# Layer-norm transposes, row sums and transposed reciprocals as column strips of 32

## The chip, the core and the metric

The kernel runs on one core of a Trainium2 chip. TensorE (PE in the profile) multiplies matrices, ScalarE (ACT) takes the exponentials, VectorE (DVE) does element-wise work, GpSimd (POOL) and SyncE (SP) mostly start transfers. The metric is the device time of one execution in microseconds; lower is better. Three runs of the kernel before gave 2268.7, 2272.3 and 2274.1 us, median 2272.32.

## The reference

Four transformer attention blocks follow each other on an input of 2048 tokens by 640 features, with 32 heads of 20 features. Blocks 0 and 2 use windowed causal attention (256 keys back), blocks 1 and 3 see all keys.

```python
def block(x, wqkv, wo, windowed):
    h = (x - mean(x)) / sqrt(var(x) + 1e-5)        # per token
    q, k, v = split_heads(h @ wqkv)                # 32 heads of 20
    s = q @ k.T * 20 ** -0.5
    if windowed:
        s = where((i - j >= 0) & (i - j < 256), s, -1e9)
    return x + merge_heads(softmax(s) @ v) @ wo
for w in (A, B, A, B):
    x = block(x, w.wqkv, w.wo, windowed=(w is A))
```

## The kernel before, in words

All four blocks are woven into one stream that is written out when the program is built. The outer loop goes over *tiles* of up to three banks of scores (128 keys by 512 queries each). In each turn TensorE writes the scores of one tile (line 1305), ScalarE takes exponentials (line 1336), and TensorE multiplies older exponentials by the values (line 1369). Scores alternate between two sets of banks, so TensorE may be about one tile ahead of ScalarE.

A *unit* is four heads by 512 queries. Four heads lie side by side in one matrix of 128 partitions, each in 32 of them: 20 or 21 are used. So scores use 32 rows of TensorE's array ("32*128" in the profile), the values use 21 columns ("128*21"), and the helper `by_columns` (line 297) splits all projections into four column strips of 32 ("128*32").

Between the scores and the values of a turn, `pump` lets *tasks* advance by a planned credit: the layer norm `t_ln`, projections, the tails of finished units. The heat counter adds filler matmuls (`unread`, which calls `by_columns` on the identity and a mask) wherever the planned work of TensorE is low, to keep its clock up. All of this is fixed when the program is written out; nothing is chosen at run time. Within an engine the order is the program's, and between engines semaphores bind.

Three places matter for the change.

- `t_ln` (transposes at line 432) normalises 128 tokens into `xn`, writes filler into the bank, turns the five 128-column pieces of `xn` around by TensorE, and `evac` copies them into `xnT`. There are 15 such layer norms of four groups of tokens; the first layer norm has its own code and isn't changed.
- `t_tail`, first step (line 1042): for one or two finished units, a matmul with four columns (`sel4`) per head group and 128 queries picks the row sums out of `oT`. VectorE takes reciprocals `rz` and splits them into a high and a low part in `hl`.
- `t_tail`, second step (line 1059): `hl` is transposed into `rp`, copied to `rT`, and later spread over the partitions (line 1080) and multiplied in (line 1084).

Of the kernel before, what the change touches and what calls it, by code (L numbers as in the profile page):

```python
# [15 lines left out]
P = 128  # L16
# [30 lines left out]
def kernel(  # L47
# [10 lines left out]
    nc = tc.nc  # L58
# [33 lines left out]
    ident = big.tile([P, P], BF16, name="ident", tag="ident")  # L92
    nhalf = big.tile([P, 4], F32, name="nhalf", tag="nhalf")
    sel4 = big.tile([P, 4], BF16, name="sel4", tag="sel4")
# [21 lines left out]
    for h in range(2):  # L116
        for n in range(2):
            a = n * D + h * HD
# [10 lines left out]
    def load_wop(w, dense):  # L129
# [9 lines left out]
        out=ident[:], in_=ident[:], compare_op=ALU.not_equal, fill=1.0,  # L139
# [6 lines left out]
    for m, b, ge in (  # L146
# [6 lines left out]
            out=v, in_=v, compare_op=ALU.is_ge if ge else ALU.is_gt, fill=0.0,  # L153
# [109 lines left out]
    def take_m():  # L263
        while True:
            b = min(mfree, key=mfree.get)
            if mfree[b][0] <= state["tick"]:
                mfree[b] = (1 << 30, 0)
                return b
            yield ("wait", 1)

    def drop_m(b):
        mseq[0] += 1
        mfree[b] = (state["tick"] + (not state["early"]), mseq[0])
# [19 lines left out]
    def by_columns(out_, lhsT, rhs, start, stop):  # L293

        for j in range(4):
            r = slice(32 * j, 32 * j + 32)
            nc.tensor.matmul(out_[r], lhsT=lhsT[:, r], rhs=rhs, start=start, stop=stop)  # L297
# [4 lines left out]
    def room(*tags):  # L302
        while any(live[t] + tags.count(t) > cap[t] for t in tags):
            yield ("wait", 1)
        for t in tags:
            live[t] += 1
        state["running"].holds = True
# [8 lines left out]
    def evac(out_, in_):  # L316
        if state["act"]:
            nc.scalar.copy(out=out_, in_=in_)
        else:
            nc.vector.tensor_copy(out=out_, in_=in_)  # L320
# [7 lines left out]
    def get_w(l, n, c, i):  # L328

        t = wqkp.tile([P, KD, P], BF16, name="wqk", tag="wqk")  # L330
        wtick[l, n, c, i] = state["tick"] + 4
        if l or c:
            a = n * D + i * P
            nc.gpsimd.dma_start(out=t[:], in_=wq_view[l % 2][:, :, a : a + P])
            return t
        tv = t[:].rearrange("p c (j m) -> p c j m", j=4)
        nc.gpsimd.memset(tv[:, :, :, DH:32], 0.0)
        src = raw[:, :, n * D + 80 * i : n * D + 80 * (i + 1)]
        nc.vector.tensor_copy(
            out=tv[:, :, :, 0:DH], in_=src.rearrange("p c (j e) -> p c j e", j=4)  # L340
        )
        wtick[l, n, c, i] = 0
        return t
# [46 lines left out]
    def t_ln(l, c):  # L390
        while ("x", l, c) not in ready:
            yield ("wait", 1)
        yield from room("xnT", "ln")
        for n in (1, 0):
            order = worder[l, n]
            if order and not any(e in wtiles for e in order):
                wtiles[order[0]] = get_w(*order[0])
        users[l, c] = 9 if (l, c) == (0, 0) else (11, 12, 11, 11)[l]
        mv = mvs.pop((l, c))
        rstd = lnp.tile([P, 4], F32, name="rstd", tag="rstd")  # L400
        nc.gpsimd.tensor_scalar(  # L401
            out=rstd[:], in0=mv[:, :, 1], scalar1=EPS, scalar2=1.0, op0=ALU.add, op1=ALU.mult
        )
        nc.gpsimd.tensor_tensor(out=rstd[:], in0=rstd[:], in1=nhalf[:], op=ALU.pow)
        yield ("wait", 2)
        nmr = lnp.tile([P, 4], F32, name="nmr", tag="nmr")
        nc.vector.scalar_tensor_tensor(
            out=nmr[:], in0=mv[:, :, 0], scalar=-1.0, in1=rstd[:], op0=ALU.mult, op1=ALU.mult
        )
        xt = xtp.tile([P, KD, C], BF16, name="xnT", tag="xnT")  # L410

        def normed(i):
            xn = xnp.tile([P, D], BF16, name="xn", tag="xn")
            nc.vector.tensor_scalar(
                out=xn[:], in0=x_sb[:, 4 * c + i, :],
                scalar1=rstd[:, i : i + 1], scalar2=nmr[:, i : i + 1],
                op0=ALU.mult, op1=ALU.add,
            )
            return xn

        rows = deque([normed(0)])
        yield ("wait", 1)
        for i in range(4):
            if i < 3:
                rows.append(normed(i + 1))
            xn = rows.popleft()
            mb = yield from take_m()
            for _ in range(1+(l<2)):
                unread(mb)
            trp = ps[:, mb, :].bitcast(BF16)[:, 0 : KD * P].rearrange("p (c m) -> p c m", c=KD)  # L430
            for dc in range(KD):
                nc.tensor.transpose(  # L432
                    out=trp[:, dc, :], in_=xn[:, dc * P : (dc + 1) * P], identity=ident[:]
                )
            evac(xt[:, :, i * P : (i + 1) * P], trp)
            drop_m(mb)
            yield ("pe", 0.4)
        xnT[l, c] = xt
        live["ln"] -= 1
        ready.add(("xnT", l, c))  # L440
# [192 lines left out]
    def unread(b):  # L633

        by_columns(ps[:, b, :], ident, masks[:, 0, :], True, True)
        state["heat"] += 1.0

    def warm_bank(b):

        if cool() and (  # L640
            state["credit"] <= 0.0 or all(task.wake > state["tick"] for task in todo)
        ):
            unread(b)
# [379 lines left out]
    def t_tail(us):  # L1023
        final = us[-1][0:3] == (3, NC - 1, G - 1)

        def fill(count):

            for n in range(count * final):
                nc.tensor.matmul(
                    ps[:, 0, :], lhsT=ident[:], rhs=masks[:, 0, :], start=True, stop=True  # L1030
                )

        n = len(us)
        yield ("wait", 2)
        fill(2)
        mb = yield from take_m()
        warm_bank(mb)
        zp = ps[:, mb, 0 : 16 * n]
        for i, (l, c, g, oT) in enumerate(us):
            for qb in range(4):  # L1040
                a = 16 * i + 4 * qb
                nc.tensor.matmul(  # L1042
                    zp[:, a : a + 4], lhsT=oT[:, qb * P : (qb + 1) * P],
                    rhs=sel4[:], start=True, stop=True,
                )
        rz = rzp.tile([P, 2, 16], F32, name="rz", tag="rz")[:, 0:n, :]
        nc.vector.reciprocal(out=rz.rearrange("p u r -> p (u r)"), in_=zp)
        drop_m(mb)

        hl = rzp.tile([P, 2, 2, 16], BF16, name="hl", tag="hl")[:, 0:n]  # L1050
        nc.vector.tensor_copy(out=hl[:, :, 0, :], in_=rz)
        nc.vector.tensor_tensor(out=hl[:, :, 1, :], in0=rz, in1=hl[:, :, 0, :], op=ALU.subtract)
        yield ("pe", 0.25)
        fill(3)
        yield ("wait", 2)
        mb = yield from take_m()
        warm_bank(mb)
        rp = ps[0 : 32 * n, mb, :].bitcast(BF16)[:, 0:P]
        nc.tensor.transpose(
            out=rp, in_=hl.rearrange("p u n r -> p (u n r)"), identity=ident[:]  # L1060
        )
        rT = rzp.tile([64, P], BF16, name="rT", tag="rT")
        nc.vector.tensor_copy(out=rT[0 : 32 * n], in_=rp)
        drop_m(mb)
        yield ("pe", 0.1)
        fill(1)
        yield ("wait", 2 if state["tick"] < last_tick[0] else 1)
        for i in range(n):
            yield from scaled(*us[i], 32 * i, rT, fill)
        if any(packed(l, c) for l, c, g, oT in us):  # L1070
            yield ("wait", 2)
        for u in us:
            yield from settle(*u)
# [121 lines left out]
    with tc.manual_schedule():  # L1195
# [14 lines left out]
        n = 0  # L1210
        last_layer = sum(len(u.banks) for u in units[: index[3, 1, 0, None]])
        placed = {}
        while n < last_layer:
            size = 2 if len(tiles) % 2 and narrow(banks[n][0]) else 3
            u = banks[n][0]
# [52 lines left out]
        while ended is None or t < ended + 8:  # L1268
# [3 lines left out]
            if t < len(tiles) or banks:  # L1272
# [9 lines left out]
                for b in cur:  # L1282
                    u = b[0]
# [18 lines left out]
                for n in range(2):  # L1302
                    for i, (u, j, m, b0, subs, first, last, end) in enumerate(cur):
                        for kc, q0, qn, col in subs[n : n + 1]:
                            nc.tensor.matmul(  # L1305
                                sp[:, i, col * P : (col + qn) * P],
                                lhsT=u.k(kc, j), rhs=u.q(j, q0, qn), start=True, stop=True,
# [22 lines left out]
                i = 0  # L1330
                while i < n_b:
                    b0 = cur[i][3]
                    k = i
                    while k < n_b and cur[k][3] == b0:
                        k += 1
                    nc.scalar.activation(  # L1336
                        out=pt[:, i:k, b0 * P :], in_=sp[:, i:k, b0 * P :],
                        func=ACT.Exp, scale=SCALE,
                    )
                    i = k  # L1340
# [5 lines left out]
                r = rate(t)  # L1346
# [6 lines left out]
            for n in range(2 if n_b == 0 or t > closed + 1 else 0):  # L1353
                u = pts[0][3][0] if pts else None
# [11 lines left out]
                for m, (kc, q0, qn, col) in enumerate(subs):  # L1366
                    for _, pg, i, b in group:
                        j = b[1]
                        nc.tensor.matmul(  # L1369
                            op[32 * j : 32 * j + VW, q0 * P : (q0 + qn) * P],  # L1370
                            lhsT=u.v(kc, j), rhs=pg[:, i, col * P : (col + qn) * P],
                            start=(first and m == 0), stop=(last and m == len(subs) - 1),
                            skip_group_check=u.windowed,
                        )
                if end and u.aside:
                    pair = side_done(u)
                    for n, j in enumerate(u.aside):
                        nc.tensor.matmul(  # L1378
                            op[32 * j : 32 * j + VW, :], lhsT=u.v(NT - 1, j),
                            rhs=pair[n // 2][:, n % 2, :], start=False, stop=True,  # L1380
# [12 lines left out]
            if t > 0 and masked is not None:  # L1393
                cur_, pt_ = masked
                i = 0
                while i < len(cur_):
# [4 lines left out]
                    if m == 1 and cur_[0][0].l == 0:  # L1401
                        for b in (1, 2):
                            if b < b0:
# [3 lines left out]
                                out=v, in_=v, compare_op=ALU.is_gt if b == 1 else ALU.is_ge, fill=0.0,  # L1407
# [3 lines left out]
                    elif m is not None:  # L1411
# [5 lines left out]
                            out=pt_[:, i:k, cols], in0=pt_[:, i:k, cols], in1=mv_, op=ALU.mult  # L1417
                        )
                    i = k
# [36 lines left out]
```

The softmax here doesn't subtract the row's maximum and nothing guards it: scores larger than these inputs give would overflow.

## Time and profile before

| what | value |
|---|---|
| span of the profiled execution | 2267.0 us |
| TensorE busy | 1973.3 us (87%) |
| ScalarE busy | 2166.5 us (96%) |
| VectorE busy | 1269.8 us (56%) |
| mean granted TensorE clock | 0.993 |
| exponentials, line 1336 | 1,636 instructions, 2089.3 us |
| transposes, line 432 | 300 matmuls, 28.4 us |
| row sums, line 1042 | 512 matmuls, 22.7 us |
| transposed reciprocals, line 1059 | 65 matmuls, 15.8 us |

A line of the profile's timeline gives the start and the time up to the last end of one or more instructions of one kind, the engine, the line, and what is written from what is read. A shape such as `128*32 128x512` means 128 rows and 32 columns of the array in use, with a moving operand of 128 partitions by 512 elements. Busy times of TensorE include the way through the array, which overlaps with what follows; the distance between starts tells what a matmul costs the next one.

### The profile page before, as it was taken

The numbers are of one execution on the slowest core, as the hardware profiler recorded it, in microseconds if no ns is written. First come the engines' busy times: TensorE is split into PE (matmuls) and PEld (weight loads), VectorE is DVE, ScalarE is ACT, GpSimd is POOL, SyncE is SP. The second block draws the span as 40 slices with busy tenths as digits, with TensorE's granted clock in tenths as the row PEclk, the third lists the DMA queues.
The fourth block names the chain that finished last, engine by engine and source line by source line (L and its number), as shares of the span: only waits on it lengthen the run. The fifth ranks groups of instructions, "written<-read, shape, count | busy, mean of one in ns | idle before, by whom it ended". The sixth has DMA issues, their size and how long they took to land.

```text
span 2267.0 us, 65801 instructions
## 1 busy us (share of the span) xinstructions
PE 1973.3 (87%) x28523; PEld 776.0 (34%) x28524; DVE 1269.8 (56%) x2158; ACT 2166.5 (96%) x1740; POOL 326.2 (14%) x571
## 2 busy tenths in 40 slices
PE   8999998988888888888888988898888888888887
PEld 3444343334333333333333443342322222222222
DVE  6766575435554565555564644442566666656665
ACT  7789899999999989999899999999999999999998
POOL 4454334201100122001210022002000000000000
PEclk9999999999999999999999999999999999999999
DMA  6233223422210233002330033103211111111100
GB/s 195 72 91 94 74 87 93 100 76 50 78 34 15 60 88 104 17 28 58 93 90 15 16 106 105 31 17 91 65 51 31 31 40 34 31 31 43 42 21 16
DMA packets 88384, 136.80 MB, mean 60 GB/s; under 512 B 20766, under 2 KB 63486, under 8 KB 88094
## 3 DMA queue, kind: packets, MB, share of 16 engines
q1 hardware_dynamic: 68878, 79.43, 12.6%
q0 software_dynamic: 19216, 53.17, 8.0%
q8 instruction: 223, 3.65, 0.7%
q14 instruction: 67, 0.55, 0.1%
HBM read 99.52 MB, written 27.79 MB: 56 GB/s over the span
## 4 chain that ended last, share of the span: by engine, by line
ACT 49%; PE 23%; issue 17%; DVE 9%; POOL 1%; DMA 1%; SPq 0%; ACTq 0%; DVEq 0%; POOLq 0%
ACT pt L1336 47%; PE ps L297 14%; PE ps L1305 5%; PE ps L1369 2%; DVE pt L1416 1%; ACT ka L1336 1%; DVE x_sb L562 1%; DVE st L320 1%; DVE on L1084 1%; PE ps L432 1%; PE ps L1080 0%; DVE vs L320 0%; DVE va L320 0%; PE ps L1042 0%; DVE raw_o L909 0%
## 5 line engine op out<-in xcount | busy, mean ns | idle before, releaser
L1336 ACT ACTIVATE pt<-ps 128x1536 bf16<-128x1536 f32 (+2 forms) x1636 | 2089.3, 1462 | 64.8 <-PE ps L1305 56.2
L297 PE MATMUL ps<-masks,ident 128*32 128x512 bf16 x6452 | 553.2, 388 | 113.2 <-ACT pt L1336 59.1
L1305 PE MATMUL ps<-qt,kt 32*128 32x512 bf16 x4004 | 545.7, 384 | 85.5 <-ACT pt L1336 77.6
L1369 PE MATMUL ps<-pt,vt 128*21 128x512 bf16 x3844 | 392.2, 382 | 0.1
L1305 PEld LDWEIGHTS <-kt 32*128 32x128 bf16 x4004 | 163.4, 91 | 544.1 <-issue 526.8
L297 PEld LDWEIGHTS <-ident 128*32 128x32 bf16 x6452 | 162.0, 94 | 361.6 <-issue 350.4
L1416 DVE TENSOR_TENSOR pt<-pt,masks 128x1024 bf16<-128x1024 bf16 (+6 forms) x331 | 191.0, 604 | 154.9 <-ACT pt L1336 154.1
L297 PE MATMUL ps<-xnT,wqk 128*32 128x512 bf16 x3320 | 221.7, 385 | 17.1 <-DVE st L320 7.9
L320 DVE CAST st<-ps 128x512 bf16<-128x512 f32 x134 | 92.6, 691 | 188.1 <-PE ps L297 187.7
L909 DVE TENSOR_SCALAR xnT<-ps 128x512 int32<-128x512 f32 x92 | 63.6, 691 | 191.4 <-PE ps L902 191.3
L297 PE MATMUL ps<-wop,on 128*32 128x320 bf16 x3712 | 156.9, 301 | 13.3 <-DVE x_sb L562 8.4
L1305 PE MATMUL ps<-qa,ka 32*128 32x384 bf16 (+2 forms) x1408 | 117.9, 276 | 32.0 <-ACT pt L1336 29.4
L1369 PEld LDWEIGHTS <-vt 128*21 128x21 bf16 x3956 | 102.5, 91 | 110.4 <-issue 64.8
L1084 DVE TENSOR_TENSOR on<-on,ps 128x512 bf16<-128x512 bf16 x128 | 86.3, 683 | 67.0 <-PE ps L1080 65.3
L297 PE MATMUL ps<-wv,xnT 128*32 128x320 bf16 x2560 | 112.4, 301 | 10.8 <-DVE on L1084 3.3
L297 PEld LDWEIGHTS <-wqk 128*32 128x32 bf16 x3320 | 79.1, 96 | 112.8 <-issue 59.4
L562 DVE TENSOR_TENSOR x_sb<-x_sb,ps 128x320 bf16<-128x320 bf16 x120 | 58.0, 483 | 104.9 <-PE ps L297 104.7
L297 PEld LDWEIGHTS <-on 128*32 128x32 bf16 x3712 | 92.8, 96 | 65.9 <-issue 49.2
L856 DVE CAST on<-ps 128x512 bf16<-128x512 f32 x112 | 77.0, 687 | 59.9 <-PE ps L1378 32.9
L401 POOL TENSOR_SCALAR rstd<-mv 128x4 f32<-128x4 f32 x15 | 3.8, 253 | 712.4 <-DVE mv L388 702.8
L1305 PEld LDWEIGHTS <-ka 32*128 32x128 bf16 x1408 | 43.2, 92 | 117.0 <-issue 110.9
L1369 PE MATMUL ps<-pt,va 128*21 128x384 bf16 (+2 forms) x1408 | 76.9, 281 | 4.6 <-POOL pt L1406 3.5
(100 smaller groups left out, 1589.8 us busy)
## 6 DMA issues: line engine op xcount, KB each, us to landing
vt<-v_d SPq DMA_DIRECT2D x48, 336.0 KB
kt<-k_d SPq DMA_DIRECT2D x192, 80.0 KB
wqk<-in_B_wqkv_dram POOLq DMA_DIRECT2D x80, 160.0 KB, 3.6
wqk<-in_A_wqkv_dram POOLq DMA_DIRECT2D x70, 160.0 KB, 3.3
k_d<-st POOLq DMA_DIRECT2D x75, 128.0 KB, 2.2
q_d<-st POOLq DMA_DIRECT2D x75, 128.0 KB, 2.2
qt<-q_d SPq DMA_DIRECT2D x384, 20.0 KB
v_d<-vs POOLq DMA_DIRECT2D x16, 336.0 KB, 3.4
```

The costliest lines, as they stand in the source:

```text
L297: nc.tensor.matmul(out_[r], lhsT=lhsT[:, r], rhs=rhs, start=start, stop=stop)
L320: nc.vector.tensor_copy(out=out_, in_=in_)
L401: nc.gpsimd.tensor_scalar(out=rstd[:], in0=mv[:, :, 1], scalar1=EPS, scalar2=1.0, op0=ALU.add, op1=ALU.mult)
L432: nc.tensor.transpose(out=trp[:, dc, :], in_=xn[:, dc * P : (dc + 1) * P], identity=ident[:])
L562: nc.vector.tensor_tensor(out=xv, in0=had, in1=yp, op=ALU.add)
L856: nc.vector.tensor_copy(out=oT, in_=op)
L909: V.tensor_scalar(out=xi.bitcast(I32)[:, i * C : (i + 1) * C], in0=side["psum"], scalar1=SCALE * LOG2E * E23, scalar2=-128.0 * E23, op0=AL ...
L1084: nc.vector.tensor_tensor(out=oT, in0=oT, in1=zb, op=ALU.mult)
L1305: nc.tensor.matmul(sp[:, i, col * P : (col + qn) * P], lhsT=u.k(kc, j), rhs=u.q(j, q0, qn), start=True, stop=True,)
L1336: nc.scalar.activation(out=pt[:, i:k, b0 * P :], in_=sp[:, i:k, b0 * P :], func=ACT.Exp, scale=SCALE,)
L1369: nc.tensor.matmul(op[32 * j : 32 * j + VW, q0 * P : (q0 + qn) * P], lhsT=u.v(kc, j), rhs=pg[:, i, col * P : (col + qn) * P], start=(first ...
L1416: nc.vector.tensor_tensor(out=pt_[:, i:k, cols], in0=pt_[:, i:k, cols], in1=mv_, op=ALU.mult)
```

## The change

The three kinds of matmuls that used all columns of the array (or 64 of them) are written as strips of 32 columns, as the projections, the filler and the values are already. Its purpose is that TensorE keeps one shape where it goes from filler to transposes or from tails to values. The products are the same; a transpose of 128 columns becomes four of 32, a row-sum matmul becomes four, and the transposed reciprocals of two units become one strip for each unit.

```diff
@@ t_ln
             for dc in range(KD):
-                nc.tensor.transpose(
-                    out=trp[:, dc, :], in_=xn[:, dc * P : (dc + 1) * P], identity=ident[:]
-                )
+                for j in range(4):
+                    a = dc * P + 32 * j
+                    nc.tensor.transpose(
+                        out=trp[32 * j : 32 * j + 32, dc, :], in_=xn[:, a : a + 32],
+                        identity=ident[:],
+                    )
@@ t_tail, row sums
                 a = 16 * i + 4 * qb
-                nc.tensor.matmul(
-                    zp[:, a : a + 4], lhsT=oT[:, qb * P : (qb + 1) * P],
-                    rhs=sel4[:], start=True, stop=True,
-                )
+                by_columns(zp[:, a : a + 4], oT[:, qb * P : (qb + 1) * P], sel4[:], True, True)
@@ t_tail, transposed reciprocals
         rp = ps[0 : 32 * n, mb, :].bitcast(BF16)[:, 0:P]
-        nc.tensor.transpose(
-            out=rp, in_=hl.rearrange("p u n r -> p (u n r)"), identity=ident[:]
-        )
+        for i in range(n):
+            nc.tensor.transpose(
+                out=rp[32 * i : 32 * i + 32], in_=hl[:, i].rearrange("p n r -> p (n r)"),
+                identity=ident[:],
+            )
```

## The prediction

> **What bounds the kernel now.** I read the busy line of each engine first, then the shares of the chain that ended last, then who waits for whom, and last the chain and TensorE's own order around the three places that change.
>
> The page's busy lines and its chain (part 1 and part 4; times in us, share of the span, number of instructions):
>
> ```profile
> PE 1973.3 (87%) x28523; PEld 776.0 (34%) x28524; DVE 1269.8 (56%) x2158; ACT 2166.5 (96%) x1740; POOL 326.2 (14%) x571
> ...
> ACT 49%; PE 23%; issue 17%; DVE 9%; POOL 1%; DMA 1%; SPq 0%; ACTq 0%; DVEq 0%; POOLq 0%
> ```
>
> ScalarE is 96% busy, nearly all with the exponentials of line 1336; TensorE is second. The waits say how the two hand the lead to each other (waiter, line waited for, us in total, times, longest):
>
> ```profile
> PE ps L1305 <- ACT pt L1336: 107.1, 332, 1.0
> PE ps L297 <- ACT pt L1336: 59.1, 126, 0.9
> ACT pt L1336 <- PE ps L1305: 56.2, 114, 2.2
> ```
>
> TensorE stands 166 us for ScalarE, and ScalarE 56 us for TensorE. So ScalarE leads over most of the span, and TensorE's time counts only in stretches where it has fallen behind. By stretch: in 0 to 300 us ScalarE is busy 249 of 300 us, in 300 to 900 us 585 of 600, in 1500 to 2256 us 751 of 756. The 56 us is about the most that any relief of TensorE can return directly.
>
> The changed groups (busy us, mean ns of one, then idle):
>
> ```profile
> L432 PE MATMUL ps<-ident,xn 128*128 128x128 bf16 x300 | 28.4, 228 | 1.2 <-DVE xn L414 1.2
> L1042 PE MATMUL ps<-sel,on 128*128 128x4 bf16 x512 | 22.7, 166 | 0.7 <-DVE st L320 0.5 <-DVE raw_o L593 0.2
> L1059 PE MATMUL ps<-ident,hl 128*64 128x128 bf16 x63 | 15.3, 243 | 1.0 <-DVE st L320 1.0
> ```
>
> These durations hold the way through the array, which overlaps with the next matmul; the cost is read from start to start, in TensorE's timeline (start, us, what):
>
> ```profile
> 323.16 0.62 PE L297 MATMUL ps<-masks,ident 128*32 128x512 bf16 x8
> 323.70 0.45 PE L432 MATMUL ps<-ident,xn 128*128 128x128 bf16 x5
> ...
> 308.26 0.35 PE L1042 MATMUL ps<-sel,on 128*128 128x4 bf16 x8
> 308.54 0.40 PE L1369 MATMUL ps<-pt,vt 128*21 128x512 bf16 x4
> ...
> 310.93 0.24 PE L1059 MATMUL ps<-ident,hl 128*64 128x128 bf16 x1
> 311.11 0.40 PE L1369 MATMUL ps<-pt,vt 128*21 128x512 bf16 x4
> ```
>
> "128*32" means that an instruction uses all 128 rows of the array and 32 columns. Four such strips run at once: the eight of 323.16 start as four at 323.156 to 323.166 and four at 323.382 to 323.393, so four strips with 512 columns of moving data take 0.22 us. The second four would be through at 323.60, but the 128*128 transposes start at 323.70: about 0.1 us is lost where the shape changes. The same loss stands after the eight of L1042: they start 25 ns apart, the last at 308.447, and the strips of L1369 start at 308.540. Over all changes of shape without a semaphore wait the trace's median gap is 93 to 106 ns. I use 95.
>
> **What the Trainium skill says.** "TensorEngine Tiling (Array Packing)", Key Properties: changing the tiling mode, not just the tile, drains TensorE. The trace agrees: 95 ns at a change, 0 to 4 ns between strips. "TensorE: Matmul & The Clock Gate", Part 3, lets tiles of one mode start about 4 ns apart; here they start 2 to 4 ns apart. The same page, Part 1, has a floor of about 25 ns between starts however small the moving side is; the 25 ns of L1042 agree for full matmuls, and no row of before shows small strips. Its weight path section ties the fast load to 128 columns, so strips lose it; the records show no longer load, 95 ns for 32 columns against 98 for 128.
>
> **The change part by part.** ScalarE's, VectorE's, GpSimd's and SyncE's instructions keep kinds and order; the filler matmuls, planned when the program is written out, stay too. Four places on VectorE wait for ScalarE as well, for work that is long done by then: nothing. On TensorE 2,499 loads with as many matmuls come on top (900 + 1,536 + 63), mostly starting in the shadow of the three strips beside them. TensorE has issued at 19 ns per instruction over 400 in a row, and a fuller issue queue is no bound as long as matmuls average 35 ns per instruction: nothing.
>
> I went along TensorE's order and noted the shape before and after each block.
>
> - Transposes, L432: 60 blocks of 5. 45 lie between strips, 15 between strips before and score matmuls (32 rows) after. Changes gone: 45 x 2 + 15 = 105, by 95 ns: -10.0 us. The transposes themselves start 56 ns apart; four strips with 128 moving columns also do (first four of line 1369 at 302.444, second four at 302.500). So 5 x 56 ns stays.
> - Row sums, L1042: 65 blocks, 44 between strips, 18 with strips after only, 2 with strips before only, 1 beside full-array filler: 108 changes, -10.3 us. Against it 8 matmuls become 8 fours. Best case 25 ns a four, as now. Worst by the nearest row: the weights of four strips were loaded and used between 302.446 and 302.508, 62 ns a four, which gives 8 x (62 - 25) = 0.3 us a block, 19 us in all. I take 37 ns, since the loads should overlap with the 25 ns floor: +0.1 us x 64 = +6.4 us.
> - Transposed ends, L1059: 33 blocks between strips, 29 with strips on one side, 3 with neither: 95 changes, -9.0 us. One 64-column matmul took 174 ns up to the next start, so 80 without the change; two strips take 56: -24 ns x 63 = -1.5 us.
>
> TensorE's sum: -29.3 + 6.4 - 1.5 = -24 us (-31 to -12).
>
> What of it lies on the path? The chain of waits shows such blocks (start, us, what):
>
> ```profile
> 335.13 0.29 PE ps L1042 x8
> 335.42 0.33 PE ps L1369 x4
> ...
> 337.40 0.17 PE ps L1059
> ```
>
> Counted over the span, 38 of the 60 transpose blocks, 26 of 65 row-sum blocks and 16 of 65 ends lie on it. With 1.75, 1.66 and 1.46 changes a block that is 38 x 1.75 x 0.095 = 6.3, 26 x 1.66 x 0.095 = 4.1 and 16 x 1.46 x 0.095 = 2.2: 12.6 us at most. The chain won't shorten one for one, because ScalarE runs just beside it. So I went along the trace with a rule: each change gone puts TensorE ahead, a wait for ScalarE at the scores or filler takes the lead away, and only where ScalarE waited for TensorE first is the lead passed on, up to that wait. It passes on 8.9 us if small strips cost nothing more, 7.2 us at 0.1 us a block, 5.4 us at 0.3 us. More than half comes before 500 us, where ScalarE has its gaps. I take 7.2: 2272.3 - 7.2 = 2265.
>
> **The rivals.**
>
> - Hidden (0.22): the relieved TensorE only waits more for ScalarE. For it: 166 us of such waits, and a ScalarE at 99% after 1500 us. Against it: 85 us of the span before 1500 us in which ScalarE is not busy. Also, TensorE's granted clock fell to half seven times between 91 and 2088 us, for 3.4 to 6.8 us each; one such dip more costs up to 1.7 us of TensorE's work. A gain of 1 to 2 us is left: 2271.
> - Slower (0.10): the floor of 25 ns holds for each small strip. Then 32 x 25 = 0.8 us stands for 0.2: 64 x 0.6 = +38 us, less the 10.3 us of changes, +28 us on TensorE. If half passes on, +14, less 0.3 x 20.5 = 6 of the other two parts: 2280. Against it: all strips seen start 2 to 4 ns apart.
> - The whole chain shortens (0.06): 12.6 us and no new wait: 2260.
>
> My forecast, part of the saving passed on, has 0.62.
>
> **How the numbers follow.** The case of 0.62 spans 2262 to 2269 with the cost of small strips, and nearly all of it is under 2267.8, which is 0.2% down: with the whole chain 0.65 for faster. Hidden and the forecast's upper edge give 0.25 for no difference; slower 0.10. The range leaves out the lower half of the last rival and most of the slow one: 2259 to 2275.
>
> **What would show it.** After: no gap of 95 ns between filler and transposes; transposes, sums and ends under the line of the strip helper; row-sum fours 25 to 62 ns apart, which settles the largest unknown; TensorE's wait for ScalarE up by 10 to 20 us, ScalarE's for TensorE down by some 5. Wrong would be fours of 100 ns, a gap that stays though both sides are strips, or more dips of the clock.

## The result and the profile after

The changed kernel took 2262.07 us (median of 4 runs, 2257.4 to 2263.83) against 2273.11 us for the kernel before (4 runs, 2268.7 to 2274.12). The ratio is 0.9952 with a 95% interval of 0.9931 to 0.9973. Two later comparisons of the same pair (e1 and e12 below) gave 0.9963 (0.9951 to 0.9974; 22 runs) and 0.9975 (0.9961 to 0.9989; 7 runs). So the measured gain is 6 to 11 us; the forecast was 7 us less, 2265 us.

The busy line and the chain's shares of the changed kernel's page:

```profile
PE 1949.7 (86%) x31022; PEld 778.5 (34%) x31023; DVE 1269.8 (56%) x2158; ACT 2163.5 (96%) x1740; POOL 324.8 (14%) x571
...
ACT 51%; PE 21%; issue 16%; DVE 10%; POOL 1%; DMA 1%; ACTq 0%; SPq 0%; DVEq 0%; POOLq 0%
```

TensorE has 2,499 matmuls more and is busy 23.6 us less; all other engines have the same count of instructions. Its share of the chain fell from 23 to 21%, ScalarE's rose from 49 to 51%. The groups that took the place of the old ones (line, operation, shapes, count, busy us and mean ns):

```profile
L434 PE MATMUL ps<-ident,xn 128*32 128x128 bf16 x1200 | 28.6, 225 | 1.6 <-DVE xn L414 1.6
L297 PE MATMUL ps<-sel,on 128*32 128x4 bf16 x2048 | 24.8, 166 | 0.9 <-DVE st L320 0.5 <-ACT xnT L318 0.2 <-DVE raw_o L596 0.2
L1060 PE MATMUL ps<-ident,hl 128*32 128x128 bf16 x128 | 14.8, 223 | 1.1 <-DVE st L320 1.1
```

Four times as many matmuls have nearly the same busy time (the row sums 2.1 us more), because the busy time of concurrent strips is counted once. TensorE's timeline at one site of each kind (start, us, what):

```profile
319.80 0.61 PE L297 MATMUL ps<-masks,ident 128*32 128x512 bf16 x8
320.24 0.45 PE L434 MATMUL ps<-ident,xn 128*32 128x128 bf16 x20
...
303.68 0.36 PE L297 MATMUL ps<-sel,on 128*32 128x4 bf16 x32
303.90 0.40 PE L1371 MATMUL ps<-pt,vt 128*21 128x512 bf16 x4
...
306.34 0.23 PE L1060 MATMUL ps<-ident,hl 128*32 128x128 bf16 x2
306.35 0.44 PE L1371 MATMUL ps<-pt,vt 128*21 128x512 bf16 x4
```

At these sites, eight filler strips held TensorE for 0.54 us before, until the transposes started; now they hold it for 0.44 us, which is their streaming time. The row sums hold it for 0.22 us in place of 0.28. Over all 63 blocks of two units, the groups of four strips start 25 ns apart in the median, 48 ns at most.

Where strips follow without a wait, the median distance from a block's first start to the next matmul fell from 383 to 279 ns for the transposes (37 sites), from 283 to 224 ns for the row sums (45 sites) and from 173 to 7 ns for the reciprocals (36 sites). The last figure flatters, because the reciprocals use two of the four strips. At the 35 sites where four strips follow, two of these start 7 and 11 ns after the block's first start, and the other two 56 and 60 ns after it; before, all four started at 173 to 183 ns. Over the whole trace TensorE changes shape 3,362 times in place of 3,670, the 308 of the prediction.

The waits of TensorE for ScalarE and the other way round (waiter, line, us, times, longest):

```profile
PE ps L1307 <- ACT pt L1338: 115.7, 356, 1.0
PE ps L297 <- ACT pt L1338: 64.9, 146, 0.9
ACT pt L1338 <- PE ps L1307: 56.5, 107, 2.7
```

The first two rose from 166 to 181 us. TensorE is busy 23.6 us less, but the profiled execution is only 5.0 us shorter. So 18.6 us went into idle time, 14 of them into these two waits for ScalarE. The third line didn't fall, though the span did. In the profile of e1, the same kernel at a granted clock of 0.994 in place of 0.991, it is 51.0 us, so dips of the clock are the likely reason.

### The profile page after: what moved, and what is told of

The parts are those of the page before. It is cut to its first block, busy times and chain, and to the rows that moved or that the text cites. A ratio compares the mean times of both kernels' runs of the same rounds, so it can differ in the third digit from the quotient of the medians.

```text
span 2262.0 us, 70803 instructions
## 1 busy us (share of the span) xinstructions
PE 1949.7 (86%) x31022; PEld 778.5 (34%) x31023; DVE 1269.8 (56%) x2158; ACT 2163.5 (96%) x1740; POOL 324.8 (14%) x571
## 4 chain that ended last, share of the span: by engine, by line
ACT 51%; PE 21%; issue 16%; DVE 10%; POOL 1%; DMA 1%; ACTq 0%; SPq 0%; DVEq 0%; POOLq 0%
ACT pt L1338 49%; PE ps L297 14%; PE ps L1307 4%; PE ps L1371 2%; DVE pt L1418 1%; ACT ka L1338 1%; DVE st L320 1%; DVE on L1086 1%; DVE x_sb L565 1%; DVE va L320 1%; PE ps L434 0%; PE ps L1082 0%; DVE xnT L320 0%; DVE vs L320 0%; DVE raw_o L912 0%
## 5 line engine op out<-in xcount | busy, mean ns | idle before, releaser
L1338 ACT ACTIVATE pt<-ps 128x1536 bf16<-128x1536 f32 (+2 forms) x1636 | 2087.2, 1472 | 63.4 <-PE ps L1307 56.5
L297 PEld LDWEIGHTS <-on 128*32 128x32 bf16 x5760 | 118.1, 96 | 78.3 <-issue 55.3
L297 PEld LDWEIGHTS <-xnT 128*32 128x32 bf16 x2560 | 63.5, 95 | 48.6 <-issue 37.7
```

The costliest lines, as they stand in the source:

```text
L1338: nc.scalar.activation(out=pt[:, i:k, b0 * P :], in_=sp[:, i:k, b0 * P :], func=ACT.Exp, scale=SCALE,)
```

## The experiments

ScalarE, VectorE and GpSimd keep their instruction counts in all of them. Beside the measured ratio to the kernel before, the table has the gain at equal granted clock. This is worked out from the runs. Over all runs of the twelve kernels and of the kernel before, a clock of 0.001 less goes with 1.56 us more (one slope for all), and the times of each kernel and of the kernel before are set to a clock of 0.992 with it. The standard error of a gain is 0.2 to 0.6 us. The kernel before is at 2270.8 us by this count, on each of the three chips used within 0.1 us. What a kernel does to the clock itself is taken out by it as well, which matters for e9 and e11.

| kernel | ratio (95%) | runs | mean clock | at equal clock, us |
|---|---|---|---|---|
| e1 all three | 0.9963 (0.9951 to 0.9974) | 22 | 0.9922 | -7.6 |
| e12 all three | 0.9975 (0.9961 to 0.9989) | 7 | 0.9911 | -7.3 |
| e2 transposes | 0.9979 (0.9970 to 0.9988) | 22 | 0.9920 | -5.3 |
| e3 row sums | 0.9996 (0.9984 to 1.0008) | 13 | 0.9910 | -1.3 |
| e4 ends | 0.9993 (0.9981 to 1.0005) | 14 | 0.9916 | -2.0 |
| e5 early | 0.9981 (0.9966 to 0.9997) | 17 | 0.9914 | -5.6 |
| e6 late | 1.0002 (0.9990 to 1.0014) | 14 | 0.9920 | -0.2 |
| e7 full filler | 0.9989 (0.9977 to 1.0000) | 14 | 0.9924 | -2.1 |
| e8 rest as well | 0.9972 (0.9961 to 0.9982) | 19 | 0.9925 | -7.0 |
| e9 filler early | 0.9970 (0.9955 to 0.9985) | 6 | 0.9945 | -2.3 |
| e10 filler late | 1.0001 (0.9989 to 1.0012) | 14 | 0.9911 | -0.7 |
| e11 less filler | 0.9984 (0.9972 to 0.9997) | 14 | 0.9895 | -7.0 |

### The parts, one at a time

All three together (e1):

> All three parts, once more, as the yardstick for the parts on the same chip. Theory A (TensorE saves 95 ns for each of 308 changes of the array's shape, and passes on the part that falls where it leads): with row-sum strips now seen at 25 to 28 ns a four, the carry rule of the prediction gives 8.9 us less. Theory B (the gain is the granted clock, not the changes): the gain follows the granted clock of the runs and is near zero at the same clock.

The transposes alone (e2), the first hunk of the diff:

> Only the layer norms' transposes as strips (105 of the 308 changes gone). A: 5 us less, over half of the gain for a third of the changes, because these blocks lie mostly where TensorE leads (0 to 500 us). B: no order among the parts, all near zero at the same clock. C (what counts is only the number of changes): 3 us less, as for each third.

The row sums alone (e3), the second hunk:

> Only the row sums as strips (108 changes gone). A: 2 us less. C: 3 us less. Slow-strip rival of the prediction (0.8 us a block): 8 us more; the trace of the changed kernel already speaks against it.

The transposed reciprocals alone (e4), the third:

> Only the transposed reciprocals as one strip for each unit (95 changes gone). A: 2 us less. C: 3 us less.

The transposes give 5.3 us at equal clock, 4.8 by the plain ratio; the two others give 1.3 and 2.0 at equal clock, while their plain intervals can't tell them from nothing. The order is theory A's (5, 2, 2), not a third each, though each has about a third of the changes. The gains don't follow the clock, which is within 0.001 of the kernel before's 0.9916 in all four: B falls as the cause of the gain. It does explain most of the scatter of single runs: of e1, the runs at a clock of 0.988 took 2268.6 and 2269.3 us, the runs at 0.995 2256.8 to 2257.9.

### Early and late

The three parts written both ways, chosen by the turn of the outer loop. For e5:

```diff
+if state["tick"] < 330:
     strips of 32
+else:
     as before
```

and for e6 with `>= 330`.

> All three parts as strips, but only in the first 330 turns of the outer loop (about the first 450 us; 85 of the 308 changes gone); later blocks as before. A (passed on where TensorE leads): 5.5 us less, over half of the gain. C (only the number of changes counts): 85/308 of the gain, some 3 us.

> The same from turn 330 on (223 of the 308 changes gone). A: 3.4 us less. C: 223/308 of the gain, some 8 us.

85 changes gone early bring 5.6 us of their 8.1 (85 x 95 ns). 223 changes gone late bring nothing that can be seen, of 21 us; C would have them bring most. Where the late saving went stands in e6's waits:

```profile
PE ps L1324 <- ACT pt L1355: 115.5, 358, 1.0
PE ps L297 <- ACT pt L1355: 64.3, 144, 0.9
```

They sum to 180 us, 14 more than before the change and as many as with all three parts everywhere. The late relief only makes TensorE wait longer for ScalarE. Theory A's 3.4 us for it was too much. The traces agree: e6 and the kernel before have the same dips of the clock (stretches in which it is recorded as half) up to 800 us, and in the start of the same exponential e6 is 0.3 us ahead at 456 us and 0.7 at 786.

The same comparison of the kernel before with e1, along the span:

| before, at us | 370 | 456 | 786 | 926 | 1337 | 1756 | 2255 |
|---|---|---|---|---|---|---|---|
| e1 is ahead by us | 4.8 | 5.5 | 5.8 | 7.7 | 8.0 | 9.6 | 10.3 |

At 370 us both executions had spent 20.5 us at half clock, so the 4.8 us can be put to the change. More than half of the whole is there at 456 us. Of what comes later, 1.9 us come between 786 and 926 us, and 0.9 between 1618 and 1756: the kernel before had its clock at half for 3.4 us at 839 and at 1706 us there, and e1 hadn't. The first at least is no work of the change, since e12, the same kernel as e1, has such a dip at 836 us.

### Shape changes put back, without touching the three parts

```diff
 def unread(b):
-    by_columns(ps[:, b, :], ident, masks[:, 0, :], True, True)
+    nc.tensor.matmul(ps[:, b, :], lhsT=ident[:], rhs=masks[:, 0, :], start=True, stop=True)
     state["heat"] += 1.0
```

> The changed kernel, with each filler of four strips by 512 columns written as one full-array matmul by 512 columns (a filler's product is not used). The streaming time is the same; counted in TensorE's order there are 3902 changes of shape in place of 3362, 540 more, 51 us of TensorE's time at 95 ns each. If the change of shape is what costs (A): slower than the changed kernel, by 15 us at the carry rule's share of 0.3 and by 25 us if half is passed on. If strips as such made the gain, or the clock (B): within 3 us of the changed kernel.

It is 5.5 us slower than e1 at equal clock (ratios 0.9989 and 0.9963), where 15 to 25 were expected: the sign was right, the size far off. The shape changes do cost about what was said, as in this piece of e7's timeline:

```profile
900.16 0.38 PE L638 MATMUL ps<-masks,ident 128*128 128x512 bf16 x1
900.47 0.40 PE L1373 MATMUL ps<-pt,va 128*21 128x384 bf16 x8
```

One full-array filler of 512 columns follows another after 0.215 to 0.227 us in this trace, but the values start 0.31 us after it. Over 487 sites where another shape follows without a wait the median is 0.309 us, so a change costs 0.08 to 0.09 us here. But most of the added changes stand where TensorE waits anyway. First e1's waits, then e7's:

```profile
PE ps L1307 <- ACT pt L1338: 114.2, 352, 1.0
PE ps L297 <- ACT pt L1338: 64.9, 146, 0.9
ACT pt L1338 <- PE ps L1307: 51.0, 108, 2.1
...
PE ps L1309 <- ACT pt L1340: 76.1, 211, 1.0
PE ps L297 <- ACT pt L1340: 58.8, 134, 0.9
ACT pt L1340 <- PE ps L1309: 57.2, 118, 2.1
```

TensorE's waits for ScalarE fell to 135 us from e1's 179. 44 of the 51 us went out of waits and 7 remain, near the 5.5 measured. Place explains this too: only 45 of the 540 added changes lie before 450 us, 4.3 us at 95 ns each, and at 456 us, with 23.9 us of half clock in both executions, e7 is 3.4 us behind e1. The 495 later ones, 47 us of TensorE's time, put it at most 6.1 us further behind. The expectation of 15 to 25 us took the share passed on from blocks that lie elsewhere.

### What is left to convert

```diff
 def t_before_last(): ...
-    nc.tensor.matmul(yp, lhsT=on[0:n, b, ...], rhs=wop[0:n, b, ...], ...)
+    by_columns(yp, on[0:n, b, ...], wop[0:n, b, ...], b == 0, b == 3)
 def fill(count): ...
-    nc.tensor.matmul(ps[:, 0, :], lhsT=ident[:], rhs=masks[:, 0, :], start=True, stop=True)
+    by_columns(ps[:, 0, :], ident, masks[:, 0, :], True, True)
```

> The changed kernel, with the partial output projection before the last unit and the closing filler as strips too (13 more changes gone, 1.2 us of TensorE, nearly all at the end where ScalarE leads). A: within 1 us of the changed kernel.

It is 0.6 us from e1 at equal clock, and no better. None of the other versions beats the changed kernel by more than the measurement can tell.

### More and less of TensorE's time, without a change of shape

In these three, fillers are added or left out ahead of the transposes.

```diff
 for _ in range(1+(l<2)):
     unread(mb)
+if l < 2:       # e9; in e10: if l >= 2
+    by_columns(ps[:, mb, :], ident, masks[:, 0, :], True, True)
```

> The changed kernel with one more filler of four strips (0.216 us, no change of shape) ahead of the transposes of each of the 28 groups of tokens of layers 0 and 1 (51 to 415 us of the trace). TensorE's time up by 6.0 us where it is held to lead. A, as the late half of the change has corrected it (all of it counts before some 450 us, nothing after): slower than the changed kernel by 4 to 6 us, so about 4 us less than before the change. If place doesn't matter (a share of a third everywhere): slower by 2 us.

> The same with the 32 groups of layers 2 and 3 (535 to 1511 us): TensorE's time up by 6.9 us where ScalarE is held to lead. A as corrected: within 1 us of the changed kernel. Place doesn't matter: slower by 2 us.

```diff
-for _ in range(1+(l<2)):
-    unread(mb)
+unread(mb)
+if l < 2:
+    state["heat"] += 1.0
```

> The changed kernel with one filler of four strips in place of two ahead of the transposes of layers 0 and 1 (28 fillers, 6.0 us of TensorE's time gone; the plan still counts them, so that no other filler takes their place). A as corrected: 4 to 6 us faster than the changed kernel, if TensorE's clock holds; if the fillers are what holds it, the granted clock falls, by 0.001 for each 4.5 us at half speed, and some 1.6 us of the gain go for each 0.001.

e9 did as expected at equal clock, and e11 didn't. The plain ratios hide this, because the clock moved. With more filler early, e9 had a mean clock of 0.9945 and took the time of e12 (0.9970 and 0.9975). With less, e11 had 0.9895 and a ratio of 0.9984. The kernel before had 0.9917 on this chip. So the filler ahead of the early transposes seems to hold the clock, by 2.7 standard errors in each direction. At equal clock e9 is 5.0 us slower than e12, of the 6.0 added. e11, for which 4 to 6 us less were expected, is 0.3 us from e12, within the error.

The traces show the same without an adjustment. At 456 us the profiled executions of e1, e9 and e11 have each spent 23.9 us at half clock. In the start of the same exponential, e9 is then 6.0 us behind e1, all that was added; e11 is 0.3 us ahead, of 6.0 taken off. TensorE's idle time before 456 us is 43.8 us in e1 and 48.3 in e11; the increase is spread over waits for the layer norm's `xn` and for ScalarE. So the corrected theory A, that all of TensorE's time before some 450 us counts, failed for time taken off the changed kernel. Perhaps the change has used up what TensorE could pass on at these blocks; that is argued, not shown.

e10 is a plain miss: 6 us slower than e12 where at most 1 was expected. Set beside e8, which had the same dips of the clock before 400 us in its profiled execution (at 50, 90, 220, 244, 258 and 381 us), it is 7.0 us behind in the start of the same exponential by 1756 us. Steps of about 2 us each lie at dips which e8 didn't have (579 and 1343 us) and one of about 1 us in its favour at one that only e8 had (838 us); so 4 to 5 of the 6.9 us were passed on directly. So theory A's "nothing after some 450 us" failed for time that is added: early and late alike, adding TensorE's time to the changed kernel costs most of what is added. TensorE's slack at the late transposes may be smaller than the filler's 0.216 us. That is argued, not shown; the slack of single blocks wasn't tried.

The last yardstick (e12):

> The changed kernel again, as the yardstick on the same chip: 7 to 9 us less than before.

## Why the prediction was right, step by step

- **308 changes at 95 ns**: right. The number agrees with the trace, and the gap is gone at the sites. Two groups of filler strips start 215 or 226 ns apart in the trace after, so up to 11 ns go without a change too, more than the 0 to 4 that the prediction read. e7, which puts such gaps into other places and leaves the three parts alone, gives back most of the gain.
- **Small strips at 37 ns a four, +6.4 us on TensorE**: too dear. They start 25 ns apart, the best case of the two bounds. A block's distance to the next strips fell from 283 to 224 ns; with 95 ns for the change taken off it would be 188, so the strips cost 36 ns a block, an estimate of 2.3 us over 64 blocks. TensorE's sum is then nearer its lower end of -31 us than the -24 taken. The slower rival, 25 ns for each strip, fell with that.
- **Transposes at 56 ns for four, ends at 56 ns for two**: right for the first: 279 ns for five fours. For the ends it held for two of the four strips that follow, while the other two start beside them after 7 and 11 ns.
- **The share passed on**: right in the sum, in part by luck. The rule gave 8.9 us with strips that cost nothing and 7.2 at the cost assumed; 7.3 and 7.6 were measured at equal clock. Two errors met in this. The strips were cheaper than assumed, so that the rule would have said over 8 us; and of the 3.4 us that it had for the late blocks, nothing was seen when they were changed alone. For the parts it gave 5, 2 and 2; they measured 5.3, 1.3 and 2.0. The early blocks gave 5.6 for 5.5. The parts sum to 8.6 us, which their errors allow. The halves sum to 5.8, 1.8 less than the whole and about three times the error of this difference. What the late blocks add when the early ones are changed too is left open.
- **Hidden**: true for the change's late blocks, after some 450 us, and false for its early ones. That is how both the rival and the forecast had a part in it.
- **The waits**: TensorE's for ScalarE rose by 14 us, in the forecast's 10 to 20. ScalarE's for TensorE was to fall by 5; it stayed at 56.5 us in the first profile, whose clock (0.991) was lower than before's (0.993), and fell to 51.0 in e1's, at 0.994.
- **What would show it**: the gaps went and the fours are 25 ns apart, as said. Only the row sums stand under the line of the strip helper, though; the transposes and the ends have lines of their own, 434 and 1060.

## What to carry to other kernels

Changes of the array's shape are read as a gap between starts that exceeds the streaming time, and can be counted in TensorE's order. Here groups of four strips of 32 started as close together as full matmuls had, 25 ns, even with four moving columns. But what such a saving is worth is decided by the stretch it falls in: here 85 early changes carried most of the gain and 223 late ones on their own turned into waits for ScalarE. And it has a limit there too: from the changed kernel, a further 6.0 us taken off early brought nothing that could be measured. For differences of a few us, record the granted clock of each run and compare at equal clock before a cause is named.

## What the hardware showed

- The granted clock varies between executions of one program: among the 59 runs of the kernel before that went with e1 to e4 it lay between 0.987, with 2278.5 us, and 0.996, with 2264.2 and 2265.8 us. It explains most of the scatter; after taking it out, the standard error of e1's mean falls from 0.95 to 0.22 us.
- The dips to half clock last 3.4 us or a small multiple of it (17.1 at most) and come back at the same places in different kernels: 13 of the 14 profiled executions have one that starts within 88 to 91 us, and several one near 1640 and 1875 us. Where one execution had a late dip of 3.4 us and the other hadn't, 1 to 2 us came in.
- After transposes in two strips, two of the four strips that follow start within 11 ns and the other two within 60 ns, at the median of 35 sites. Before, with one transpose in 64 columns, all four started after 173 to 183 ns.
